# A fixed order for the first five groups of a gated recurrence and its feed-forward part

## The chip, the cores and the metric

The kernel runs on one core of one Trainium2 chip. The metric is the time of one execution on the device in microseconds (us); a median is taken over several executions. The profiled execution also has a span, from the first to the last instruction on the core, some 2 us shorter than the time of the run.

In the profile PE is the tensor engine, PEld its weight loads, DVE the vector engine, ACT the scalar (activation) engine, POOL the GpSimd engine and SP the engine that issues most transfers.

## The reference, cut to what matters

A recurrence over 768 time steps for 4 batches and 8 heads of width 48, with a complex decay `a`, feeds a gated two-layer product:

```python
a = a * min(|a|, 0.999) / (|a| + 1e-6)          # normalised complex decay
for t in range(S):                              # q, k, v: (4, 8, 768, 48)
    S_re, S_im = a_re*S_re - a_im*S_im + k[t] v[t]^T,  a_re*S_im + a_im*S_re
    y[t] = q[t] @ S_re
x = y.transpose(0, 2, 1, 3).reshape(3072, 384)
out = (sigmoid(x @ w_gate) * (x @ w_val)) @ w_out   # 384 -> 1536 -> 384
```

## The kernel before

The sequence is cut into 24 slabs of 128 steps, and the slabs into ten groups, numbered from 0. A group goes through five parts. `prep_0`: square of `a` on ACT, sum and clip on POOL. `prep_a`: logarithms and decays (ACT, PE, POOL), with a round trip of one row of decays through DRAM. `prep_b`: angles, sine and cosine (ACT), and the rotated q and k (DVE). `attn`: the attention within the slab. Then the dense work: `gateval` (36 matmuls for the gate and 36 for the value, whatever the size of the group) and `outproj` (12 matmuls for each slab).

```python
SIZES = [1, 2, 3, 3, 3, 3, 3, 3, 2, 1]

def prep_0(g):
    nc.scalar.activation(out=sq[:, :, :n], in_=G.a2[:, :, :n], func=FT.Square)
    for s in range(n):
        nc.gpsimd.tensor_tensor(out=G.lm[:, s], in0=sq[:, 0, s], in1=sq[:, 1, s], op=ALU.add)
        G.last_pool = nc.gpsimd.tensor_scalar(out=G.lm[:, s], ...)
        yield

def prep_a(g):
    nc.scalar.preload_act_table_set("natural_log_exp_and_others")
    nc.scalar.activation(out=ar, in_=ar, func=FT.Ln)
    nc.scalar.activation(out=lm, in_=lm, func=FT.Ln)
    ...
        nc.tensor.matmul(cl, wl_t, G.lm[:, s], start=True, stop=True)
        ...                                     # ee = exp(+-cl)
        nc.sync.dma_start(scr[b][c:c + 1], ee[L - 1:L, 0])
        ...                                     # rbe <- scr, a column for each slab
        if c > 0:
            nc.vector.tensor_tensor(out=arr[b][:, c - 1], in0=rbe[b][:, c - 1],
                                    in1=rbe[b][:, c], op=ALU.mult)
        nc.gpsimd.tensor_tensor(out=G.qk[:, :, s], in0=G.qk[:, :, s], in1=ee, op=ALU.mult)
        yield
```

`merge` interleaves generators by their share of steps done. ACT's order is fixed by the program; the other engines are ordered by the scheduler. The main loop runs three things side by side: the attention of group i, the preparation of group i+1, and the dense work of older groups.

```python
with tc.manual_schedule(engines={ACT}):
    ...
    run_all(prep_0(0)); run_all(prep_a(0)); run_all(prep_b(0))     # cut to one line
    run_all(prep_0(1))
    with tc.issue_after(gs[1].last_pool.ins):
        load_weights()                           # gate, value, then output weights
    for i in range(NG + 2):
        st = []
        if i + 2 < NG:
            loads_a(i + 2)
            loads_q(i + 2)
        if i < NG:
            at = attn(i)
            ...
            st.append((take(at, n1), n1))        # 2/5 of the attention
        if 0 <= i - 2:
            st.append((outproj(i - 2), 3 * sz(i - 2)))
        if i + 1 < NG:
            st.append((prep_a(i + 1), 1 + sz(i + 1)))
        merge(*st)
        st = []
        if i < NG:
            st.append((at, na - n1))
        if 0 <= i - 1 < NG:
            st.append((gateval(i - 1), 2 * NFB))
        if i + 1 < NG:
            st.append((prep_b(i + 1), 1 + 2 * sz(i + 1)))
        if i + 2 < NG:
            st.append((prep_0(i + 2), sz(i + 2)))
        merge(*st)
```

## Time and profile before

| | value |
|---|---|
| time, median of 3 runs | 340.59 us (337.92 to 340.93) |
| span of the profiled run | 336.2 us, mean granted clock 0.939 |
| table load that opens prep 3, 4, 5, 6 | 87.12, 119.94, 151.65, 185.16 us |

The last row is a ruler ("prep 3" is the preparation of group 3). Each preparation begins with a load of ACT's logarithm table (1.28 us). ACT's order is fixed, so its start tells how far a kernel is: in a kernel that runs the loop, the load of prep i+1 opens the stage of attention i. The prediction shows how the slices and stages read; here are the busy sums and the clock, first from the page's first part, then from its slices (tenths of full speed).

```profile
PE 269.7 (80%) x2328; PEld 176.8 (53%) x2328; DVE 214.4 (64%) x385; ACT 221.2 (66%) x377; POOL 164.0 (49%) x177
...
PEclk9997856569897999999999999999999999999999
```

PE is busy for 269.7 of 336.2 us, and the clock is 0.5 to 0.6 in slices 6 to 9 (42 to 76 us), where PE is busy for 16.44 of 33.6 us. The lines of PE and DMA by slice, the table by stage and ACT's timeline before stand in the prediction.

### The profile page before, as it was taken

How to read it: one execution, taken by the hardware profiler on the slowest of the kernel's cores; microseconds unless marked ns; L12 is line 12 of the kernel's file. 1: busy time of each engine (PE TensorE's matmuls, PEld its weight loads, DVE VectorE, ACT ScalarE, POOL GpSimd, SP SyncE). 2: the span in 40 equal slices, each digit the busy share in tenths (PEclk: the TensorE clock that was granted, in tenths of full speed). 3: DMA queues.
4: the chain of work that ended last, by engine and by line, in shares of the span. 5: the costliest groups of instructions: out<-in, count | busy, mean ns of one | idle time of the engine just before them, and what ended most of it. 6: DMA issues, size and time to landing. Idle time of an engine off the chain costs nothing.

```text
span 336.2 us, 6365 instructions
## 1 busy us (share of the span) xinstructions
PE 269.7 (80%) x2328; PEld 176.8 (53%) x2328; DVE 214.4 (64%) x385; ACT 221.2 (66%) x377; POOL 164.0 (49%) x177
## 2 busy tenths in 40 slices
PE   0443546087959897999899989998999999999995
PEld 0122233064736664666555646565666666666874
DVE  2021262738874975896489648966886798576633
ACT  5665084275878399759875887497756956764443
POOL 2489473928296629934863486248423612400000
PEclk9997856569897999999999999999999999999999
DMA  7999997992991299559614970483023100100110
GB/s 140 189 151 194 189 197 131 165 165 27 163 179 13 55 163 184 71 94 187 127 23 82 184 136 3 75 151 61 2 47 96 26 0 26 48 2 23 49 47 26
DMA packets 152383, 32.70 MB, mean 97 GB/s; under 512 B 144905, under 2 KB 152353, under 8 KB 152353
## 3 DMA queue, kind: packets, MB, share of 16 engines
q1 hardware_dynamic: 148368, 28.76, 52.6%
q0 software_dynamic: 3984, 3.54, 6.4%
q8 instruction: 18, 0.29, 0.4%
q14 instruction: 13, 0.10, 0.1%
HBM read 31.07 MB, written 4.76 MB: 107 GB/s over the span
## 4 chain that ended last, share of the span: by engine, by line
PE 45%; ACT 19%; DVE 8%; DMA 8%; POOL 7%; issue 6%; SPq 4%; ACTq 0%; DVEq 0%; POOLq 0%
PE pg L377 9%; PE pv L382 8%; PE po L396 8%; DMA a<-in_a_im_dram 6%; PE cl L196 4%; PE ct L230 4%; SPq L117 3%; POOL qk L211 3%; PE ct L233 2%; DVE qst L257 2%; ACT L184 2%; ACT a L220 2%; DMA scr<-ee 2%; ACT L219 2%; PE tp L308 2%
## 5 line engine op out<-in xcount | busy, mean ns | idle before, releaser
L377 PE MATMUL pg<-xt,wg 128*128 128x384 f16 (+2 forms) x360 | 67.8, 297 | 6.7 <-ACT g L385 3.4
L382 PE MATMUL pv<-xt,wv 128*128 128x384 f16 (+2 forms) x360 | 68.7, 296 | 3.7 <-DVE p L386 2.7
L385 ACT ACTIVATE g<-pg 128x384 f16<-128x384 f32 (+2 forms) x120 | 49.0, 429 | 32.7 <-PE pg L377 31.1
L386 DVE SCALAR_TENSOR_TENSOR p<-g,pv 128x384 f16<-128x384 f16 (+2 forms) x120 | 54.6, 467 | 19.7 <-ACT g L385 16.0
L396 PE MATMUL po<-wo,p 128*128 128x384 f16 x288 | 55.5, 326 | 0.0
L311 DVE COPY qkT<-tp 128x1024 f16<-128x1024 f16 x48 | 32.5, 687 | 32.0 <-PE tp L308 31.7
L211 POOL TENSOR_TENSOR qk<-qk,ee 128x768 f32<-128x768 f32 x24 | 44.5, 1876 | 2.6 <-ACT ee L199 2.4
L171 POOL TENSOR_TENSOR lm<-sq 128x384 f32<-128x384 f32 x24 | 26.0, 1098 | 40.4 <-ACT sq L168 39.9
L377 PEld LDWEIGHTS <-wg 128*128 128x128 f16 x360 | 32.4, 99 | 24.3 <-issue 13.1
L382 PEld LDWEIGHTS <-wv 128*128 128x128 f16 x360 | 32.4, 99 | 19.0 <-issue 7.4
L323 DVE TENSOR_TENSOR mst<-sc,msk_t 128x512 f16<-128x512 f32 x48 | 32.4, 682 | 7.6 <-PE sc L319 7.6
L196 PE MATMUL cl<-lm,wl_t 128*128 128x384 f32 x48 | 24.7, 604 | 15.6 <-ACT lm L186 13.6
L244 DVE TENSOR_SCALAR r<-ct 128x384 f16<-128x384 f32 x24 | 13.2, 550 | 37.1 <-PE ct L233 19.1
L230 PE MATMUL ct<-a,wt_t 128*128 128x384 f32 x48 | 24.3, 592 | 14.2 <-ACT a L220 14.2
L396 PEld LDWEIGHTS <-p 128*128 128x128 f16 x288 | 26.1, 98 | 13.2 <-issue 0.2
L307 PE MATMUL tp<-idn_t,kst 128*128 128x128 f16 x192 | 30.2, 233 | 3.2 <-DVE kst L257 3.2
L257 DVE TENSOR_TENSOR kst<-qk,cs 128x768 f16<-128x768 f32 x24 | 24.5, 1023 | 12.7 <-ACT cs L253 12.2
L189 POOL TENSOR_TENSOR a<-a 128x384 f32<-128x384 f32 x24 | 23.8, 1016 | 16.6 <-ACT a L187 16.4
L308 PE MATMUL tp<-idn_t,qst 128*128 128x128 f16 x192 | 29.5, 232 | 1.7 <-DVE qst L257 1.7
L224 POOL TENSOR_SCALAR v<-v 128x384 f16<-128x384 f32 x24 | 14.0, 583 | 28.6 <-PE y L336 21.5
L289 POOL CAST x<-u 128x384 f16<-128x384 f32 x20 | 11.0, 552 | 34.0 <-DVE u L283 21.5
L339 ACT ACTIVATE y<-y 128x384 f16<-128x384 f32 x24 | 11.8, 490 | 23.2 <-PE y L336 23.1
(54 smaller groups left out, 511.2 us busy)
## 6 DMA issues: line engine op xcount, KB each, us to landing
a<-in_a_re_dram SPq DMA_DIRECT2D x24, 192.0 KB
a<-in_a_im_dram SPq DMA_DIRECT2D x24, 192.0 KB
qk<-in_q_dram SPq DMA_DIRECT2D x24, 192.0 KB
qk<-in_k_dram SPq DMA_DIRECT2D x24, 192.0 KB
v<-in_v_dram SPq DMA_DIRECT2D x24, 192.0 KB
out_dram<-ot SPq DMA_DIRECT2D x24, 192.0 KB
wg<-in_moe_w_gate_dram POOLq DMA_DIRECT2D x3, 384.0 KB, 9.7
wv<-in_moe_w_val_dram POOLq DMA_DIRECT2D x3, 384.0 KB, 11.4
```

What stands on the lines that cost most here:

```text
L196: nc.tensor.matmul(cl, wl_t, G.lm[:, s], start=True, stop=True)
L211: nc.gpsimd.tensor_tensor(out=G.qk[:, :, s], in0=G.qk[:, :, s], in1=ee, op=ALU.mult)
L230: nc.tensor.matmul(ct, wt_t, th[:, s], start=True, stop=False, skip_group_check=True)
L257: nc.vector.tensor_tensor(out=dst.rearrange("p h (r x) -> p h r x", r=2)[:, :, :, 0:D], in0=G.qk[:, 1 - i, s].rearrange("p (h d) -> p h d" ...
L308: nc.tensor.transpose(tp[:, i], G.qs[s][:, h], idn_t)
L311: nc.vector.tensor_copy(out=qkT, in_=tp)
L323: nc.vector.tensor_tensor(out=mst, in0=sc, in1=msk_t.unsqueeze(1).broadcast_to([L, 4, L]), op=ALU.mult)
L377: nc.tensor.matmul(pg, wg16[:, j, fc], G.xt[:, j, :nt], start=(j == 0), stop=(j == 2))
L382: nc.tensor.matmul(pv, wv16[:, j, fc], G.xt[:, j, :nt], start=(j == 0), stop=(j == 2))
L385: nc.scalar.activation(out=g16, in_=pg, func=FT.Tanh, scale=0.5)
L386: nc.vector.scalar_tensor_tensor(out=G.p[:, fb, :nt], in0=g16, scalar=1.0, op0=ALU.add, in1=pv, op1=ALU.mult)
L396: nc.tensor.matmul(po, G.p[:, fb, s * L:(s + 1) * L], wo16[:, fb], start=(fb == 0), stop=(fb == NFB - 1))
```

## The change

Its intent: the gate and value weights should land between the loads of groups 2 and 3 (a tiny transfer, the gate, reads the last value weights, so that the sync queue holds back later loads), and each of the early groups should go through its dense work right after its attention. The sync order becomes fixed by the program, the sizes become 1, 2, 2, 3, ..., 3, 1, and the output weights are issued later. The core of the diff:

```diff
-    SIZES = [1, 2, 3, 3, 3, 3, 3, 3, 2, 1]
+    SIZES = [1, 2, 2, 3, 3, 3, 3, 3, 3, 1]
...                                    (load_weights split into load_gv and load_out;
...                                     the cast of v moved behind each slab's q/k)
-    with tc.manual_schedule(engines={ACT}):
+    with tc.manual_schedule(engines={ACT, SP}):
...
-            load_weights()
-        for i in range(NG + 2):
+            load_gv()
+        merge((attn(0), 7), (seq(prep_a(1), prep_b(1)), 8))
+        gate = dram.tile([1, 64], F16, name="gate", bufs=1, tag="gate")
+        nc.sync.dma_start(gate, wv16[0:1, 2, DFF - 64:DFF])
+        loads_a(2)
+        loads_q(2)
+        merge((attn(1), 14), (gateval(0), 24))
+        run_all(prep_0(2))
+        with tc.issue_after(gs[2].last_pool.ins):
+            load_out()
+        loads_a(3)
+        loads_q(3)
+        merge((prep_a(2), 3), (outproj(0), 3))
+        merge((prep_b(2), 5), (gateval(1), 24))
+        loads_a(4)
+        loads_q(4)
+        merge((attn(2), 14), (outproj(1), 6))
+        run_all(prep_0(3))
+        run_all(prep_a(3))
+        merge((prep_b(3), 7), (gateval(2), 24))
+        run_all(prep_0(4))
+        for i in range(3, NG + 2):
...
-            if 0 <= i - 2:
-                st.append((outproj(i - 2), 3 * sz(i - 2)))
+            go = max(i - 2, 2)
+            st.append((outproj(go), 3 * sz(go)))
+            if i == 4:
+                st.pop()
...
-            if 0 <= i - 1 < NG:
+            if 3 <= i - 1 < NG:
                 st.append((gateval(i - 1), 2 * NFB))
```

More of the change, by code (lines that the diff above doesn't have):

```diff
@@ L14 @@
 ACT = mybir.EngineType.Activation
+SP = mybir.EngineType.SP
 RCONST = 1.5 * 2.0**23
@@ L141, with load_gv @@
     wo16 = const.tile([128, NFB, DM], F16, name="wo16")
-    def load_weights():
+    def load_gv():
         for f in range(0, DFF, 512):
@@ L148, in load_weights, with load_out @@
                     src[:, f:f + 512].rearrange("(j p) f -> p j f", p=128))
+    def load_out():
         for j in range(0, NFB, 4):
@@ L222, in prep_b @@
         G.qs, G.ks = [], []
-        for s in range(n):
-            nc.gpsimd.tensor_scalar(out=G.v16[:, s], in0=G.v32[:, s],
-                                    scalar1=YSC, scalar2=1.0,
-                                    op0=ALU.mult, op1=ALU.mult)
         yield
@@ L264, in prep_b @@
             G.ks.append(ks)
+            nc.gpsimd.tensor_scalar(out=G.v16[:, s], in0=G.v32[:, s],
+                                    scalar1=YSC, scalar2=1.0,
+                                    op0=ALU.mult, op1=ALU.mult)
             yield
@@ L426, in sz, with seq @@
         return len(GROUPS[g])
-    with tc.manual_schedule(engines={ACT}):
+    def seq(*its):
+        for it in its:
+            yield from it
+    with tc.manual_schedule(engines={ACT, SP}):
         nc.scalar.preload_act_table_set("natural_log_exp_and_others")
@@ L437 @@
         run_all(prep_b(0))
-        run_all(prep_0(1))
+        p0 = prep_0(1)
+        run_all(p0)
         with tc.issue_after(gs[1].last_pool.ins):
-            load_weights()
-        for i in range(NG + 2):
+            load_gv()
[20 more added lines that the diff above has]
+        for i in range(3, NG + 2):
             st = []
```

## The prediction

> **What bounds the kernel now.** I read the slices first, then the table by stage, then the Activation engine's timeline, the chain of waits and the DMA table. The slices divide the run in two:
>
> ```profile
> span 336.2 us, 6365 instructions
> PE   0443546087959897999899989998999999999995
> ...
> DMA  7999997992991299559614970483023100100110
> ```
>
> ```profile
> 0.00:33.00 33.00, 10.10 (x35) 5.05 (x36) 6.00 (x19) 20.31 (x26) 20.38 (x31) 0.94 1.11 168
> 33.00:41.30 8.30, 5.02 (x25) 2.59 (x23) 2.31 (x4) 0.00 (x0) 4.27 (x5) 0.82 1.23 189
> 41.30:70.00 28.70, 11.30 (x83) 7.90 (x83) 15.19 (x16) 16.39 (x23) 18.07 (x17) 0.59 1.12 167
> 70.00:110.00 40.00, 32.89 (x302) 23.24 (x303) 27.88 (x52) 29.24 (x52) 26.26 (x27) 0.87 0.73 102
> 110.00:290.00 180.00, 168.33 (x1486) 107.79 (x1485) 138.94 (x242) 132.09 (x225) 92.73 (x97) 1.00 0.49 85
> ```
>
> Columns after the length: PE, weight load, DVE, ACT, POOL busy, clock, DMA share, GB/s. From 110 us on PE is busy 168.33 of 180 us: the tensor engine is the bound. Before 70 us it works 26.4 of 70 us and DMA is full: that is where 44 us lie idle, and all that the change can win. The reason stands in the Activation timeline and the chain:
>
> ```profile
> 31.65 1.28 ACT L221 ACT_TABLE_LOAD   x1
> 41.30 2.12 ACT L168 ACTIVATE sq<-a 128x2304 f32<-128x2304 f32 x1 [8.37 <-DMA a<-in_a_im_dram]
> 43.33 0.47 ACT L250 ACTIVATE cs<-ct 128x384 f32<-128x384 f32 x1
> ```
>
> ```profile
> 23.62 17.45 DMA a<-in_a_im_dram
> ```
>
> The hand-fixed ACT order puts the square of group 2 (numbering from 0) ahead of the cosines of group 1 and group 0's output copy. The square waits for its load, so ACT does nothing from 33 to 41.3 us. The load takes 17.45 us because the weights, issued at 21.7 us, share the DMA engines:
>
> ```profile
> q1 hardware_dynamic: 148368, 28.76, 52.6%
> q0 software_dynamic: 3984, 3.54, 6.4%
> ```
>
> A packet of the weights is 3.54 MB / 3984 = 889 bytes, one of the inputs 194 bytes. The six gate and value pieces land 6.1 to 14.8 us after issue, some 2.5 us apart, the last at 40.6 us; the output weights land until 48.6 us. Between 23.6 and 49 us the sync queue needs 3 to 6 us to issue an input DMA that takes about 1 us when alone.
>
> **What the Trainium skill says.** "DMA: Bandwidth & Descriptors", section "Queues, rings and completion order": each engine goes round-robin between queues by packet. With packets 4.6 times as large the weights should get most of the bytes; the trace agrees (3.54 MB in 27 us for the weights, beside 1.18 MB of group 2's a in some 20 us). "PSUM — Partial Sum Buffer", "Engine vs sequencer instructions": the Scalar, Vector and GpSimd queues are strict FIFO; the 8.37 us wait above, with cosines behind it ready, agrees. "TensorE: Matmul & The Clock Gate", "What's actually happening": the array runs at half clock after an idle window of about 3.4 us; the clock column is 0.59 in 41 to 70 us and 1.00 after 110, so bubbles also make the matmuls beside them slower. "SBUF — State Buffer", "Who interferes with whom": DVE and GpSimd share a port pair; the update of the state takes 2.12 us at 60.24 us beside a GpSimd multiply and 0.55 us elsewhere.
>
> **The change part by part.** It removes and adds almost no arithmetic: 24 slabs as before; slab counts become 1,2,2,3,...,3,1. It adds one tiny DMA (the gate, which reads the last value weights), so that group 2's loads wait for them, and fixes the sync order. What counts is the order of the first five groups. The instruction order of the changed kernel shows ACT doing: prep 1, y of group 0, all sigmoids of group 0 and y of group 1, and only then the square of group 2; then sigmoids of group 1; then y of group 2; then prep 3 bare; and so on. I walk through it with durations of the profile before.
>
> 1. To 38 us: GpSimd issues six weight DMAs instead of nine (9 x 0.78 us ended at 28.8, now 26.5), so the arctan of group 1 starts 2.3 us sooner. The ACT hole of 8.4 us is gone. But DVE's order now has the first two products of decays (arr) before group 1's rounding and q/k products. They need a DRAM round trip (scr took 3.6 us, rbe 2.8), here beside the weights: I put 3 us on the path. q/k of group 1 ready at about 43 us (before: 50).
> 2. Attention 1 beside gate/value 0. DVE sets the length: qkT 4 x 0.69, p 12 x 0.28, mst 4 x 0.68, P, u, xt together about 11.5 us. End at 56 (before, group 1's last xt came near 86).
> 3. Prep 2, nearly bare: square 1.5, POOL 2 x (1.0 + 0.54) = 3.1, to 60.6. Only now are the output weights issued; first piece 6.1 us after issue, then 2.5 us each: 66.7, 69.2, 71.7. PE's order is cl, 8 matmuls of po (two pieces needed), cl, 4 of po; ACT's order has the copy of po before the sigmoids of group 1. So PE stands until about 69 us and the first sigmoid comes at 74.
> 4. Gate/value 1 with prep 2b: ACT 3 table loads 3.8 + arctan 0.84 + g 12 x 0.39 + cosines 2.6 = 12 us; to 86.
> 5. Attention 2 with output 0 and 1: DVE again, about 10.5 us; to 96.7.
> 6. Prep 3, almost bare: square 2.1, POOL 5.3, logs, cl, ee, table: 13.8 us with some 5 us of PE work; to 110.5.
> 7. Gate/value 2 with prep 3b: 24 x 0.33 + 3 x 1.6 = 12.7 us on PE, 13.3 on ACT; 14 us; to 124.7.
> 8. Attention 3, output 2, preps 4 and 5 without gate/value: ACT 22, DVE 21, PE 18 us; 25 us with waits; to about 150.
>
> At the next table load (start of attention 4) the kernel before stood at 151.6 us and needed 184.6 us more. What is left, in PE time: per slab gate/value 3.92 (24 x 0.49 / 3), output 1.96 (12 x 0.163), prep about 2.3 and attention about 2.4 (10.6 us of PE per slab between 151.6 and 254.5, less the first two). Before: 15 attentions, 18 gate/values, 21 outputs, 12 preps = 36 + 70.6 + 41.2 + 27.6 = 175.4. After: 16, 19, 19, 13 = 38.4 + 74.5 + 37.2 + 29.9 = 180. With the measured 184.6 / 175.4 that is 189.4 us, plus 3 for the first half of attention 4, which has no output product beside it: 192.4. Sum 150 + 192 = 342 us of span, 344 as a run (the profiled run was 338.16 against a span of 336.2).
>
> So the gain of the start (at about 86 us five slabs of attention work's inputs are ready and groups 0 and 1 are nearly through the dense part, worth some 10 us of PE) is given back in steps 3, 5, 6 and 8, where PE has only attention or only preparation to do. I shade this to 342, because the sizes look tuned and I may count two stalls that the hardware overlaps.
>
> **Rivals.** (a) The start is worth more than I think: with the weights alone on the DMA engines they could land by 36 us, PE would stay warm, and PE has 44 us of idle time to give before 70 us; no output weights stall. Then steps 1 to 8 take 138 to 142 us and the run 328 to 334. For it: idle 17.4 of 28.7 us in 41 to 70 us. Against it: the square of group 2 is now behind a whole attention. (b) The output weights become the new wait, as in step 3, up to 13 us of PE, and the bare preps leave PE cold: 350 to 356. For it: landing times of 16.7 to 20.6 us of these three DMAs in the profile before, though queued behind the others there. (c) Everything after 110 us is PE-bound and the shifts at the start only reorder the same idle time: 336 to 346. (d) The fixed sync order makes input loads stand behind outputs; I give it little, as DMA share is under 0.5 later.
>
> **Range and chances.** Rival (c) is my centre, (a) pulls down, (b) up; my walk has eight terms each uncertain by 2 to 4 us, about 9 us together. Range 326 to 356. Faster by over 2% (under 333.8) 0.26; within 2% 0.44; slower (over 347.4) 0.30.
>
> **What would show it.** Right: ACT without the hole at 33 us; gate DMA near 39 us; group 2's square near 56; a PE gap of about 13 us that ends on the output weights near 70; a bare prep 3 near 97 to 110 with PE under half busy; the eleventh slab's attention done and the table load of attention 4 near 150. Wrong: output weights landed before PE asks; PE over 90% busy already from 75 us; or attention 4 starting before 143 us, which makes it faster by over 2%.

## The result and the profile after

| | before, same rounds | after |
|---|---|---|
| time, median of 4 runs | 339.25 us (337.63 to 340.93) | 363.36 us (362.0 to 365.52) |
| ratio | | 1.0716, 95% interval 1.0631 to 1.0801 |
| span of the profiled run | 336.2 us | 360.1 us |

A ratio is the mean time of one kernel's runs over that of the other's runs of the same rounds, so it isn't quite the ratio of the medians. The change makes the kernel 7% slower, and the time lies above the predicted range. The page after, same parts as before:

```profile
span 360.1 us, 6368 instructions
...
PE 280.6 (78%) x2328; PEld 179.6 (50%) x2328; DVE 205.2 (57%) x385; ACT 222.1 (62%) x376; POOL 158.5 (44%) x177
...
PE   1354692589735977667789989998998998999996
...
PEclk9998596589955996989699999999999999999999
DMA  7979899928931299149508941992242001101011
```

The same 2328 matmuls keep PE busy for 10.9 us longer (280.6 against 269.7), at a mean granted clock of 0.905 against 0.939; the rest of the 23.9 us is 13.0 us more idle time. PE is at 90% as early as slice 6 (45 to 54 us), but falls to 20% in the next one, and from slice 11 to 20 (90 to 180 us) it is below 80% in all but one.

ACT's timeline after gives the landmarks of the prediction's walk. A bracket is the idle time just before, and what ended it:

```profile
54.85 1.48 ACT L171 ACTIVATE sq<-a 128x1536 f32<-128x1536 f32 x1
...
71.38 0.49 ACT L200 ACTIVATE ee<-cl 128x384 f32<-128x384 f32 x1 [8.35 <-PE cl L199]
...
74.46 0.66 ACT L387 ACTIVATE g<-pg 128x256 f16<-128x256 f32 x2
...
97.14 2.12 ACT L171 ACTIVATE sq<-a 128x2304 f32<-128x2304 f32 x1
...
104.77 1.16 ACT L189 ACTIVATE lm<-lm 128x1152 f32<-128x1152 f32 x1 [3.03 <-POOL lm L176]
...
128.95 2.13 ACT L171 ACTIVATE sq<-a 128x2304 f32<-128x2304 f32 x1
...
136.00 1.17 ACT L189 ACTIVATE lm<-lm 128x1152 f32<-128x1152 f32 x1 [2.44 <-POOL lm L176]
...
161.75 1.28 ACT L187 ACT_TABLE_LOAD   x1
```

The squares of groups 2, 3 and 4 stand at 54.85, 97.14 and 128.95 us, prep 5 starts at 161.75 us. The squares of groups 3 and 4 stand right ahead of their own logarithms (lm), which wait for POOL in between. The chain of waits names the transfers on the path (start, length):

```profile
24.57 4.70 DMA scr<-ee
29.29 6.10 DMA rbe<-scr
...
60.45 8.13 DMA wo<-in_moe_w_out_dram
```

The first two are the round trip of the decays, the third the output weights, as step 3 of the prediction had it. The table by stage (columns as in the prediction: length, then PE, weight load, DVE, ACT and POOL busy, clock, DMA share, GB/s):

```profile
54.90:74.40 19.50, 9.16 (x31) 4.56 (x32) 0.59 (x2) 8.61 (x12) 11.52 (x13) 0.56 1.06 164
97.10:112.40 15.30, 7.07 (x21) 3.67 (x19) 0.36 (x1) 10.72 (x13) 10.82 (x13) 0.52 0.41 66
112.40:129.00 16.60, 15.07 (x95) 10.29 (x95) 12.38 (x23) 11.63 (x26) 4.82 (x5) 0.82 0.42 63
129.00:161.80 32.80, 21.51 (x187) 13.57 (x184) 19.08 (x30) 21.22 (x31) 25.68 (x26) 0.84 0.59 94
161.80:196.40 34.60, 29.40 (x250) 17.92 (x247) 25.39 (x46) 24.40 (x40) 18.74 (x20) 0.90 0.67 95
196.40:360.10 163.70, 150.97 (x1329) 97.22 (x1326) 109.31 (x198) 106.13 (x189) 58.13 (x59) 1.00 0.32 60
```

The first two rows are the first part of prep 2 and the bare part of prep 3: DVE is busy for 0.59 and 0.36 us only, PE for less than half the time, and the clock is 0.56 and 0.52. "TensorE: Matmul & The Clock Gate" in the Trainium skill, section "What's actually happening", gives a half-rate clock after an idle window; these stages agree.

### The profile page after: what moved, and what is told of

Same layout as the page of the kernel before. It is cut to its first block, busy times and chain, and to the rows that moved or that the text cites. A ratio compares the mean times of both kernels' runs of the same rounds, so it can differ in the third digit from the quotient of the medians.

```text
span 360.1 us, 6368 instructions
## 1 busy us (share of the span) xinstructions
PE 280.6 (78%) x2328; PEld 179.6 (50%) x2328; DVE 205.2 (57%) x385; ACT 222.1 (62%) x376; POOL 158.5 (44%) x177
## 4 chain that ended last, share of the span: by engine, by line
PE 45%; ACT 21%; DVE 13%; DMA 9%; issue 7%; POOL 4%; SPq 1%; DVEq 0%; ACTq 0%; POOLq 0%
PE pg L379 9%; PE pv L384 8%; PE cl L199 6%; PE po L398 6%; PE ct L229 5%; PE ct L232 3%; ACT L222 3%; ACT a L223 2%; POOL lm L174 2%; DMA wo<-in_moe_w_out_dram 2%; DVE qst L256 2%; ACT lm L189 2%; DMA a<-in_a_im_dram 2%; DVE mst L325 2%; ACT L187 2%
## 5 line engine op out<-in xcount | busy, mean ns | idle before, releaser
L379 PE MATMUL pg<-xt,wg 128*128 128x384 f16 (+2 forms) x360 | 69.6, 302 | 8.5 <-ACT g L387 6.8
L384 PE MATMUL pv<-xt,wv 128*128 128x384 f16 (+2 forms) x360 | 70.5, 302 | 0.9 <-DVE p L388 0.8
L398 PE MATMUL po<-wo,p 128*128 128x384 f16 x288 | 57.2, 334 | 5.1 <-DMA wo<-in_moe_w_out_dram 5.1
L199 PE MATMUL cl<-lm,wl_t 128*128 128x384 f32 x48 | 27.9, 681 | 29.0 <-ACT lm L189 29.0
L214 POOL TENSOR_TENSOR qk<-qk,ee 128x768 f32<-128x768 f32 x24 | 43.6, 1836 | 10.2 <-ACT ee L202 9.7
L291 POOL CAST x<-u 128x384 f16<-128x384 f32 x20 | 10.1, 505 | 71.0 <-DVE u L285 70.8
L384 PEld LDWEIGHTS <-wv 128*128 128x128 f16 x360 | 33.3, 101 | 14.9 <-issue 2.9
L243 DVE TENSOR_SCALAR r<-ct 128x384 f16<-128x384 f32 x24 | 13.3, 552 | 34.6 <-PE ct L232 23.1
L309 PE MATMUL tp<-idn_t,kst 128*128 128x128 f16 x192 | 29.2, 229 | 2.7 <-DVE kst L256 2.5
L256 DVE TENSOR_TENSOR kst<-qk,cs 128x768 f16<-128x768 f32 x24 | 23.0, 959 | 6.1 <-ACT cs L252 4.8
L199 PEld LDWEIGHTS cl<-lm,wl_t 128*128 128x128 f32 x48 | 9.8, 244 | 33.2 <-ACT lm L189 31.8
```

The costliest lines, as they stand in the source:

```text
L256: nc.vector.tensor_tensor(out=dst.rearrange("p h (r x) -> p h r x", r=2)[:, :, :, 0:D], in0=G.qk[:, 1 - i, s].rearrange("p (h d) -> p h d" ...
L379: nc.tensor.matmul(pg, wg16[:, j, fc], G.xt[:, j, :nt], start=(j == 0), stop=(j == 2))
L384: nc.tensor.matmul(pv, wv16[:, j, fc], G.xt[:, j, :nt], start=(j == 0), stop=(j == 2))
L398: nc.tensor.matmul(po, G.p[:, fb, s * L:(s + 1) * L], wo16[:, fb], start=(fb == 0), stop=(fb == NFB - 1))
```

## The experiments

The theory that I started with: the dense products of groups 0 to 2 are used up right after their attention, so preparations 2 to 4 and attentions 2 and 3 run with little beside them. The rivals: the single waits seen above (output weights, decays), the gate, the sizes, the fixed sync order, or the place of the squares. Twelve kernels ran, all correct, each with 4 runs; those of one batch share the runs of the kernel before, whose medians were 338.92, 338.63 and 338.53 us.

### The dense work lags again from group 1 on: a_lagged

Keeps the new sizes, gate, sync order and start; from attention 1 on it runs the loop of before.

```diff
         loads_a(2)
         loads_q(2)
-        merge((attn(1), 14), (gateval(0), 24))
         run_all(prep_0(2))
         with tc.issue_after(gs[2].last_pool.ins):
             load_out()
...                              (the other lines of the fixed order are gone)
-        for i in range(3, NG + 2):
+        for i in range(1, NG + 2):   # with the stages of the loop of before
```

> Sizes, gate, sync order and order of groups 0 and 1 of preparation as in the changed kernel, but from attention 1 on the loop of the kernel before: gate/value one group behind, output two behind, prep one ahead, lm two ahead. Theory that the dense products are used up early and leave attention and prep bare: most of the 24 us come back, 335 to 345 us. Rival, gate, late loads or sync order are the cause: it stays above 354 us.

Measured: 336.33 us (335.64 to 338.3), ratio to before 0.9903 (0.9857 to 0.9948). The whole loss is gone, so it lies in the fixed order from attention 1 on, and not in the gate, the sizes or the sync queue. Its stages, with the borders at the table loads of preps 2 to 6:

```profile
46.40:76.40 30.00, 18.22 (x177) 12.99 (x176) 13.72 (x29) 18.36 (x34) 21.77 (x25) 0.80 1.00 161
76.40:106.90 30.50, 22.23 (x205) 15.91 (x203) 20.71 (x37) 23.33 (x40) 19.19 (x19) 0.94 0.91 133
106.90:139.90 33.00, 28.99 (x269) 20.01 (x266) 25.27 (x43) 23.98 (x41) 19.62 (x20) 0.95 0.69 105
139.90:172.10 32.20, 29.40 (x266) 18.63 (x262) 26.27 (x48) 25.02 (x42) 19.88 (x21) 1.00 0.70 108
172.10:336.20 164.10, 151.31 (x1331) 97.29 (x1327) 111.04 (x199) 106.11 (x190) 57.83 (x59) 1.00 0.31 60
```

Every stage but the last row, which is all the rest, holds an attention, a preparation and dense work at once, and still takes 30.0 to 33.0 us. The stages of preps 3 and 4 of the changed kernel take as long with less in them: 31.8 us (99.29 to 131.10) without an attention, and 30.7 us (131.10 to 161.75) without a gate/value. From prep 6 on the two kernels need the same: 164.1 and 163.7 us.

### Lag from group 2 on, and from group 3 on: a_lag_from2, a_lag_from3

These put a ladder between the two ends: the fixed order runs a little further each time, then the loop of before takes over.

```diff
 # a_lag_from2: the fixed order up to attention 1 beside gate/value 0 and prep_0(2), then
+        run_all(prep_a(2))
+        merge((prep_b(2), 5), (prep_0(3), 3))
+        for i in range(2, NG + 2):   # loop of before
 # a_lag_from3: the fixed order up to attention 2 beside output 1, then
         run_all(prep_0(3))
         run_all(prep_a(3))
-        merge((prep_b(3), 7), (gateval(2), 24))
-        run_all(prep_0(4))
+        merge((prep_b(3), 7), (prep_0(4), 3))
         for i in range(3, NG + 2):   # loop of before, without outputs 0 and 1
```

> The fixed order up to attention 1 beside gate/value 0, then prep 2 bare, then the loop of the kernel before from attention 2 on (gate/value 1 and outputs lag again). Dense-work theory: only the bare prep of group 2 is left of the loss, so 342 to 350 us, between the lagged kernel (336) and the changed one (363), with preps 3, 4 and 5 some 30 to 33 us apart. Rival, the loss is already made by attention 1 beside gate/value 0: 355 us or more.

> The changed kernel up to attention 2 beside output 1, then prep 3 bare (with the square of group 4), then the loop of before from group 3, so gate/value 2 lags beside attention 3 again. Lag from group 1 on gave 336.3, from group 2 on 342.5, never (the change) 363.4. Theory (each stage of attention without dense work beside it costs some 6 us): prep 3 ends near 122, table load of prep 5 near 153, and the 196.3 us that the lagged kernel needs after it: 348 to 353. Rival (the loss comes from the square and lm at the head of prep 3 and 4 alone, which this keeps for prep 3 only): 355 to 359. Rival (the loss is all made before attention 3): 361 to 365.

Measured: 342.48 us (342.3 to 343.73), ratio 1.012 (1.0082 to 1.0159), and 355.6 us (353.67 to 356.18), ratio 1.0485 (1.0434 to 1.0537). The first is inside the theory's numbers. The second is 2.6 us above them and inside those of a rival. Part of the miss is mine: I added up spans and left out the 2 us to a run. The other part is prep 5, at 156.78 us where I had 153. But the number alone can't rule the rival out, so I compare the traces at the ruler:

| kernel | load of prep 3 | prep 4 | prep 5 | span | from prep 5 to the end |
|---|---|---|---|---|---|
| a_lagged | 76.35 | 106.86 | 139.93 | 336.2 | 196.3 |
| a_lag_from2 | 80.64 | 112.90 | 144.68 | 340.2 | 195.5 |
| a_lag_from3 | 99.81 | 123.51 | 156.78 | 351.8 | 195.0 |
| after | 99.29 | 131.10 | 161.75 | 360.1 | 198.4 |

Each rung can be read where two kernels have the same work behind them, or one just a little more. a_lagged and a_lag_from2 have done the same work at prep 3: prep 2 by itself costs 4.3 us there (80.64 less 76.35), and both need 260 us from then on. a_lag_from3 at prep 4 has only output 1 (two slabs) more behind it than a_lag_from2, is 10.6 us later, and still needs 228.3 us against 227.3. The changed kernel at prep 5 has only output 2 (three slabs) more behind it than a_lag_from3, is 5.0 us later, and still needs 198.4 us against 195.0. So dense work done early was not returned by any rung: it isn't missing from a stage that would have been longer with it. What makes the time, as I read these rows, are stages in which an attention and the next preparation run one after the other. Two rows of a_lag_from3 show such a preparation alone and then a merged stage:

```profile
99.80:123.50 23.70, 10.82 (x35) 5.62 (x35) 8.92 (x9) 17.16 (x23) 21.07 (x22) 0.78 0.38 59
123.50:156.80 33.30, 25.35 (x235) 17.89 (x236) 25.76 (x46) 23.23 (x40) 21.29 (x22) 0.85 0.66 93
```

Prep 3 alone takes 23.7 us with PE busy for 10.8; the stage after it adds an attention and a gate/value to a preparation and takes only 9.6 us more.

### The squares of groups 3 and 4 one stage earlier: a_prep0_early

```diff
-        merge((prep_b(2), 5), (gateval(1), 24))
+        merge((prep_b(2), 5), (gateval(1), 24), (prep_0(3), 3))
...
-        run_all(prep_0(3))
...
-        merge((prep_b(3), 7), (gateval(2), 24))
-        run_all(prep_0(4))
+        merge((prep_b(3), 7), (gateval(2), 24), (prep_0(4), 3))
```

> The changed kernel with the square and the POOL part of prep (lm) of groups 3 and 4 merged one stage earlier, beside gate/value of groups 1 and 2. Theory of the bare chain: the logs of groups 3 and 4 start without 5 us of square and POOL work ahead of them, so prep 3 bare shrinks from 14 to about 9 us and the stage after gate/value 2 by some 4: 8 to 10 us shorter in all, 353 to 355 us. Rival, the engines are the limit there and not the chain: under 2 us.

Measured: 354.27 us (351.39 to 355.85), ratio 1.0428 (1.0365 to 1.0492): 9.1 us less than the changed kernel. The number is as expected, its division is not: I had 5 us for the bare prep 3. At the ruler prep 3 stands at 99.91, prep 4 at 130.03 and prep 5 at 157.13 us. So most of it comes after prep 4: that stage shrinks from 30.7 to 27.1 us. At prep 3 the 3.03 us wait of lm is gone, but the square only moved into prep 2b and made that longer. The bare squares are a third of the loss of 27 us against a_lagged, not all of it. Its stages of preps 3 and 4:

```profile
99.90:130.00 30.10, 22.89 (x116) 13.98 (x115) 14.51 (x24) 22.13 (x36) 17.64 (x17) 0.77 0.50 76
130.00:157.10 27.10, 19.59 (x170) 12.81 (x169) 19.02 (x29) 18.98 (x29) 21.42 (x20) 0.85 0.69 110
```

This run also settles the rival at the last rung of the ladder, and partly in its favour. a_lag_from3 moves the square of group 4 as well, and beyond that lets gate/value 2 and output 2 lag. It reaches prep 5 at 156.78 us, a_prep0_early at 157.13: 23.7 + 33.3 us for the two stages in the one, 30.1 + 27.1 us in the other. So nearly all of the 5.0 us of that rung (4.6 us) is the place of the square, and a gate/value done early costs what it costs later. At this rung early dense work by itself is then not the loss. For the rungs before it, that leaves attentions 1 and 2 and preps 2 and 3, which run one after the other. This is a comparison of stages: a kernel that merges these and keeps the dense work early was not run.

### The output weights early: a_wo_early, a_both, and the decays: a_wo_arr

`load_out()` is issued right behind `load_gv()`; a_both adds it to a_prep0_early; a_wo_arr adds it to the changed kernel and also puts each product of decays (arr) behind the q/k products of its slab on DVE.

```diff
             load_gv()
+            load_out()
...
-        with tc.issue_after(gs[2].last_pool.ins):
-            load_out()
 # a_wo_arr, in prep_b, with the arr product of prep_a removed
+            if c > 0:
+                with tc.issue_after(last.ins):
+                    nc.vector.tensor_tensor(out=arr[b][:, c - 1], ...)
```

> The changed kernel with the output weights issued right behind the gate and value weights. Output-weight theory: the second cl of group 2 no longer waits (8.35 us in the changed kernel), the first sigmoid of group 1 comes near 66 us instead of 74.5, and the run is 6 to 8 us shorter, 355 to 357 us. Rival, the gap only moves to the next bare stage or to group 2's loads, which now land later: under 2 us. Neither theory lets this alone bring back the 24 us that the change cost.

> The changed kernel with early output weights and late decay products. In the run with early output weights alone the cosines of group 1 came at 45.4 us instead of 38.7 (decays 7.8 us on the way beside more weight traffic) and gave back what the output weights saved. Theory of the two paths: with both out of the way, cosines near 34 us, first sigmoid of group 1 near 64 to 67, run 353 to 357 us. Rival, the two waits are not where the time goes: 361 us or more.

> Output weights early and the squares of groups 3 and 4 one stage earlier. Squares alone gave 354.3, output weights alone 363.1. Theory (the 1 to 2.6 us that the early output weights win are swallowed again before prep 5, where DVE and POOL set the end of attention 3): 352 to 356. Rival (they were swallowed only because of the bare square of group 4, and a 10 us wait is returned now): 343 to 349.

Measured: a_wo_early 363.06 us (361.97 to 364.82), ratio 1.0702 (1.0651 to 1.0753); a_wo_arr 361.97 us (361.15 to 363.94), ratio 1.0692 (1.0648 to 1.0735); a_both 353.85 us (351.33 to 355.95), ratio 1.0441 (1.0375 to 1.0507), against 354.27 without the early weights. The first two are misses. I took a wait on the chain of 8 us for 6 to 8 us of time. In a_wo_early it is gone, but ACT's timeline has another in its place:

```profile
45.42 0.49 ACT L249 ACTIVATE cs<-ct 128x384 f32<-128x384 f32 x1 [12.46 <-PE ct L245]
...
61.37 1.49 ACT L171 ACTIVATE sq<-a 128x1536 f32<-128x1536 f32 x1
```

The first cosines of group 1 wait 12.46 us, so the square of group 2 stands at 61.37 instead of 54.85 us. Two things add up. The decays of the second slab, now beside three more weight transfers, took 7.83 us (scr) and 6.10 us (rbe), against 6.8 us (from the issue at 30.20 us to the queue's next step at 37.00) and at most 3.1 us in the changed kernel. And in DVE's order, which the scheduler made anew, both products of decays (38.13 and 44.22 us) now stand ahead of the first rounding of group 1; in the changed kernel only the first did (36.92 us). a_wo_arr shortens that wait too and reaches prep 4 at 129.12 us, 2.0 us ahead of the changed kernel, yet prep 5 comes at 162.14, 0.4 us behind it. DVE's timeline shows a likely place, the rotated q and k of group 4:

```profile
150.85 1.12 DVE L252 TENSOR_TENSOR kst<-qk,cs 128x768 f16<-128x768 f32 x1
151.90 1.75 DVE L252 TENSOR_TENSOR qst<-qk,cs 128x768 f16<-128x768 f32 x1
...
156.39 1.75 DVE L252 TENSOR_TENSOR qst<-qk,cs 128x768 f16<-128x768 f32 x1
...
162.81 0.95 DVE L252 TENSOR_TENSOR kst<-qk,cs 128x768 f16<-128x768 f32 x1
```

From 150.4 to 160.6 us DVE has no gap, and POOL computes the lm of group 5 at the same time (151.25 to 158.5 us). A q product takes 1.75 us there, 0.95 and 1.25 us at the same place in the changed kernel. "SBUF — State Buffer", section "Who interferes with whom", has an instruction with two inputs in SBUF contend with GpSimd's reads; this agrees. That this is what ate the 2 us was not tested by itself. What is shown is that removing the two waits returned at most 1.4 us.

### Gate, decays and sizes by themselves: a_lag_nogate, a_lag_arr, b_sizes, a_lag_oldsizes

```diff
 # a_lag_nogate: a_lagged without
-        gate = dram.tile([1, 64], F16, name="gate", bufs=1, tag="gate")
-        nc.sync.dma_start(gate, wv16[0:1, 2, DFF - 64:DFF])
 # a_lag_arr: a_lagged with arr behind the q/k products, as in a_wo_arr
 # b_sizes: the kernel before with
+    SIZES = [1, 2, 2, 3, 3, 3, 3, 3, 3, 1]
 # a_lag_oldsizes: a_lagged with
+    SIZES = [1, 2, 3, 3, 3, 3, 3, 3, 2, 1]
```

> The lagged kernel without the gate DMA. The trace of the changed kernel has the sync queue reach the gate at 37.9 us, from a wait for the decays, while the last value weights landed at about 36.7: the gate then waits for nothing, and this run is within 1% of the lagged one, 334 to 339 us. Rival, the gate holds group 2's loads back: group 2's square comes earlier than 44.9 us and the time moves by 3 us or more.

> The lagged kernel with the products of decays put behind the q/k products on DVE, so that DVE no longer stands 9.3 us for their DRAM round trip. Theory of the round trip: cosines of group 1 at about 34 us instead of 39. But ACT then waits for group 2's load at 44.9 us all the same, so the run gains 0 to 3 us, 333 to 337. Rival, the round trip is on the path to the end: 5 us or more.

> The kernel before with only the slab counts of the changed one (1,2,2,3,3,3,3,3,3,1). Theory: sizes are neutral, within 1% of before, 336 to 343 us. Rival, the larger last but one group or the smaller third group costs part of the 24 us: 345 us or more.

> The lagged kernel (336.3) with the sizes of before, 1,2,3,...,3,2,1. Sizes alone were worth -0.3% in the kernel before: 335 to 340 if they are neutral here too. If the smaller third group is what makes the start of the lagged kernel short: 341 to 346, if the second last group of two makes its tail long: the new sizes better by as much.

Measured: 336.56 us, ratio 0.9924 (0.9889 to 0.9958); 336.97 us, 0.9936 (0.9897 to 0.9975); 338.06 us, 0.9967 (0.9914 to 1.0019); 336.08 us, 0.9923 (0.988 to 0.9966). All four are neutral. The gate never held anything back: the last value weights had landed at about 36.7 us in the changed kernel, while the sync queue, standing at the decays' round trip, issued the gate only at 37.9. In a_lag_arr the 8.21 us wait of a_lagged's first cosines fell to 2.78 us, and the next one, the square waiting for its load, grew from 2.14 to 7.73 us.

### The hole of the kernel before: b_sq_late

The one edit is to the kernel before: the square of group 2 goes behind the cosines of group 1.

```diff
-            if i + 2 < NG:
+            if 0 < i and i + 2 < NG:
                 st.append((prep_0(i + 2), sz(i + 2)))
             merge(*st)
+            if i == 0:
+                run_all(prep_0(2))
```

> The kernel before with one edit: the square of group 2 behind the cosines of group 1, so the ACT hole of 8.4 us is gone and nothing else. If the hole is the visible fault that the prediction took it for: 330 to 334. If it only moves to the next wait, as with the new sizes: 336 to 341.

Measured: 338.5 us, ratio 0.9995 (0.994 to 1.005). ACT's timeline:

```profile
37.62 0.49 ACT L250 ACTIVATE cs<-ct 128x384 f32<-128x384 f32 x1 [4.21 <-PE ct L246]
...
44.78 2.12 ACT L168 ACTIVATE sq<-a 128x2304 f32<-128x2304 f32 x1 [4.15 <-DMA a<-in_a_im_dram]
...
59.84 1.16 ACT L186 ACTIVATE lm<-lm 128x1152 f32<-128x1152 f32 x1 [10.46 <-POOL lm L173]
```

The cosines come 5.7 us earlier (37.62 against 43.33), then the square waits 4.15 us for its load all the same, and lm waits 10.46 us for POOL, against 1.88 us in the kernel before. At prep 3 (87.70 against 87.12 us) nothing is left. About half of the hole was there in any case: without the square in front, the cosines still wait 4.21 us for PE. So the hole that the change was aimed at was not worth 8 us, nor any.

No version beats both kernels by a margin that counts: a_lag_oldsizes, a_lagged and a_lag_nogate are 0.8 to 1.0% faster than the kernel before.

## Why the prediction was wrong

| step of the walk | predicted end, us | measured | error of the step |
|---|---|---|---|
| 1 q/k of group 1 | 43 | 44.4 | +1.4 |
| 2 attention 1 | 56 | 54.85 | -2.5 |
| 3 first sigmoid of group 1 | 74 | 74.46 | +1.6 |
| 4 gate/value 1, prep 2b | 86 | 88.0 | +1.5 |
| 5 attention 2 | 96.7 | 97.14 | -1.6 |
| 6 bare prep 3 | 110.5 | 111.1 | +0.2 |
| 7 gate/value 2, prep 3b | 124.7 | 128.95 | +3.6 |
| 8 attention 3, to prep 5 | 150 | 161.75 | +7.5 |
| what is left | 192.4 | 198.35 | +6.0 |

The error of a step is how much the distance to the prediction grew in it; they add up, but for rounding, to the 17.7 us between 342.4 and 360.1. (The 344 us of a run that this makes was then shaded to 342, which was the wrong way.)

**Right: the bare stages and the first six steps.** The gap on the output weights and the bare prep 3 are in the trace, each step within 2.6 us. Some of this is luck. In step 1 two errors cancelled: I put 3 us on the decays' round trip, and DVE stood still for 9.3 us (to 36.92); the rest of the step was shorter than I had thought. In step 2 my own durations end at 54.5, near the measured 54.85, and not at the 56 that I wrote. And the sign for the table load of attention 4 counted wrongly: by then eight slabs have their attention done, and eleven their preparation.

**Step 7** took 17.8 us in place of 14. I priced 24 matmul triples at full speed. PE was busy for 15.07 of 16.60 us, at a mean clock of 0.82. The stage came right after a bare one, and the first 5.9 us still ran at half clock, the rest at full clock:

```profile
112.40:118.30 5.90, 4.41 (x11) 2.44 (x11) 2.82 (x4) 4.78 (x7) 4.82 (x5) 0.50 0.15 1
118.30:129.00 10.70, 10.67 (x85) 7.85 (x85) 9.56 (x20) 6.85 (x19) 0.00 (x0) 1.00 0.57 97
```

So some 2.2 us (half of 4.41, an estimate) are a clock that I hadn't put in, although my own text said that bubbles slow the matmuls beside them.

**Step 8 is the largest error:** "ACT 22, DVE 21, PE 18 us; 25 us with waits". The busy sums of ACT and DVE were nearly right (21.22, 19.08), PE took 3.5 us more (21.51, at clock 0.84), but POOL isn't among them, and it is the busiest engine of the stage with 25.68 us: the lm of group 4 and of group 5 both fall in it, beside the q/k products. And the engines don't overlap there as "25 us with waits" had it: the square of group 4 (128.95) and POOL's lm come first, and the logarithm of lm only at 136.00; DVE stands still for 7.15 us up to 139.33. a_prep0_early takes prep_0 of group 4 out of the stage and shortens it by 3.6 us. The rest I put down to the chain of a preparation through five engines, which no run shortened by itself: prep 3 took 23.7 us with nothing else in its stage (a_lag_from3), and the stages with more beside a preparation took 27.1 to 34.6 us.

**What is left** was taken as PE time. I scaled 180 us of PE work with a factor from the kernel before and added 3 us for the half stage without an output product. The stage from 161.8 to 196.4 us took 34.6 us with 29.40 us of PE; in a_lagged the same stage, with the output product in it, took 32.2 us with 29.40 us of PE at clock 1.00. Early output work shortened nothing, and the stage took 2.4 us more, at a mean clock of 0.90. So the step that failed here is to count dense work done early as time saved later. From prep 6 on the two kernels need the same (163.7 and 164.1 us), with PE busy for 150.97 of 163.70.

**The rivals.** (b) came closest, 350 to 356, half for the wrong reason: the output weights were a wait on the path, yet returned 0.3 us when removed. Its other half, bare preps that leave PE cold, is in the trace (clock 0.56 and 0.52). (c), my centre, failed: the shifts at the start did not just reorder idle time, they set attentions and preparations one after the other. (d), to which I gave little, cost nothing: a_lagged keeps the fixed sync order and is no slower than the kernel before. (a) and its 44 us "all that the change can win" read idle time as something to win; b_sq_late and b_sizes show that filling the visible hole gains nothing within 1%.

What stays open is how the 27 us between the changed kernel and a_lagged divide into pure loss of overlap and low clock: PE's busy time accounts for 10.6 us of it (280.6 less 270.0), but no run held the clock apart. Whether the order of attention and preparation is the loss without the early dense work was compared, not tested. And why a_wo_arr lost its 2 us before prep 5 was read, not tested.

## What to carry to other kernels

A merged stage of attention, preparation and lagging dense work took 30.0 to 33.3 us here, where a preparation alone took 23.7. So before you move work "as soon as it can", check that the new order doesn't set two long chains of many engines one after the other that ran side by side before. Price a stage by the chain through all engines, POOL too, and by the clock that the stage before leaves, not by the largest busy sum with a few us for waits. A wait on the chain is worth its length only if nothing behind it waits for something else: here waits of some 8 us were removed or shortened in four kernels (a_wo_early, a_wo_arr, a_lag_arr, b_sq_late) and returned 1.4 us at most.

## What the Trainium skill lacked or had wrong

- "DMA: Bandwidth & Descriptors", section "Anatomy of one DMA — SWDGE (gpsimd) path", gives a fixed cost of about 2.0 us. It has no figure for how long a small transfer from the sync queue takes while weights are under way. Here 1.5 KB of decays took 4.70 us to DRAM and 6.10 us back (first slab of group 1, changed kernel); those of the second slab took 6.8 us and at most 3.1 us there, and 7.83 and 6.10 us beside three more weight transfers (a_wo_early).
